# First query block built in halves, silu moved to GpSimd, and gate rows and second modulation columns back on TensorE, in a transformer block on one core

## The chip, the cores and the metric

The kernel runs on one core of a Trainium2 chip. The metric is the device time of one execution in microseconds; the median of several runs is compared.

## What is computed

```python
def _layernorm(x, axis=-1, eps=1e-05): ...           # (x - mean) / sqrt(var + eps)
x = A_x                                              # (1, 2048, 512) bf16
mod = (_silu(c) @ w_mod).reshape(c.shape[0], 6, 1, -1)   # c (1, 512), w_mod (512, 6*512)
sa, ca, ga, sb, cb, gb = ...                         # the six slices of mod
h = _layernorm(x) * (1 + ca) + sa
x = x + ga * attention(h)       # 32 query heads of 128, 8 kv heads, the last 512 cached keys, then wo
h = _layernorm(x) * (1 + cb) + sb
x = x + gb * (relu(h @ B_w1) @ B_w2)                 # 512 -> 1792 -> 512
```

The six slices of `mod` are needed in two shapes. `sa`, `ca`, `sb`, `cb` scale and shift the transposed activations, so they are wanted as columns (feature on the partition). `ga` and `gb` multiply rows of output, so they are wanted as one row repeated on all 128 partitions.

## The kernel before

The 2048 queries are handled in four blocks of 512 (`NB`), and each block has 32 heads. One pair (block, head) is a unit; there are 128 units and one step of the main loop for each. In step s the program issues, in this order: the tasks due at s (`run_tasks`), the scores of unit s for the first two key chunks (`s_mms(s, 0)`), the query projection of unit s + 2 (`q_mms`), the scores for the other two chunks, the product of probabilities and values of unit s - 1 (`pv_mms`), and up to four entries of a background queue (`pop_bg(4)` on `bgq`). An entry marked by `evac` ends a pop: it copies the finished bank `psW` (`WBK`) out on VectorE. The background queue holds the products with `wo`, which enter it for the first time at step 9, after eight heads. The MLP follows the last unit.

Every engine works through its own stream in program order. `KB.op` records an instruction with the semaphores it must wait for; `mm` and `tpose` (lines 1367 and 1370 of the profile) issue TensorE's matmuls and transposes. All loads are issued by SyncE (SP), apart from three early ones on ScalarE's queue. `load_wm01` brings the first two slices of `w_mod` as two halves of the contraction: chunks 0 and 1 on SP, chunks 2 and 3 on ScalarE's queue. `load_wm` brings slices 2 to 5, as tasks of steps 0 to 3.

The start of the program builds the first block. `silu_exp` transposes `c` on TensorE and takes exp(-c) on ScalarE. `ln_stat` takes mean and variance of tiles 0 to 2 on VectorE (tile 3 goes through ScalarE). `rstd_pow` takes the power -0.5 on GpSimd (POOL) for tiles 0 and 1, then for 2 and 3. `silu_mul` finishes silu on VectorE with three small instructions, and its result `sc_bf` feeds 32 matmuls of one column each (`mod_cols_mm(0)`), which give the first shift and scale columns `modc`. `ln_norm` normalizes tiles 0 to 2 on VectorE; tile 3 is normalized on ScalarE. Transposes (`ln_tposes`) bring all four tiles into banks 0 and 2, with 1, 2 and 3 filler matmuls (`warm`) between the tiles. `ln_mod_ps` then scales and shifts 512 queries at a time, two feature chunks on VectorE and two on ScalarE, into `hT[0]`, and `q_mms(0)`, `q_mms(1)` project them. `q_mms` ends with a copy of the bank to `qT` on ScalarE, for which the scores wait.

The gate rows (slices 2 and 5) and the second columns (slices 3 and 4) are made without TensorE: `mod_part` multiplies and adds the four chunks of a slice on VectorE (16 instructions, steps 5 to 33), `mod_sum` adds over the partitions on GpSimd (`partition_all_reduce`, four of them), and `mod_col` takes columns from the rows of slices 3 and 4 at step 48.

Of the kernel before, what the change touches and what calls it, by code (L numbers as in the profile page):

```python
# [8 lines left out]
ACTF = mybir.ActivationFunctionType  # L9
ALU = mybir.AluOpType  # L10
# [1188 lines left out]
def build_fast(nc, es, top, A_x, A_k_cache, A_v_cache, A_wq, A_wo, B_x, B_w1, B_w2, c, w_mod, out, flag):  # L1199
# [28 lines left out]
    def T(name, shape, dt=BF):  # L1228
        return es.enter_context(nc.sbuf_tensor(name, shape, dt))
# [26 lines left out]
    ones = T("ones", [P, P])  # L1256
    c_row = T("c_row", [DC, P])
    s3 = T("s3", [P, 4], F32)
    sc_bf = T("sc_bf", [P, DC])
    sc_f = T("sc_f", [P, DC], F32)  # L1260
    tmp = T("tmp", [P, DC], F32)
    modc = T("modc", [P, 4 * DC], F32)
    gaf = T("gaf", [P, D], F32)
    gbf = T("gbf", [P, D], F32)
    prv = h2T[1][:, :, :].rearrange("p c q -> p (c q)").bitcast(F32)
    pr = [gaf[:, :], prv[:, 0:D], prv[:, D:2 * D], gbf[:, :]]
    st = T("st", [P, NT, 6], F32)
    mv = T("mv", [P, NT, 2], F32)
    rstd = T("rstd", [P, NT], F32)
# [39 lines left out]
    R_xn, R_xnT = RL("xn", TPB), Res("xnT")  # L1309
    R_yt, R_yo = RL("yt", NY), RL("yo", NY)  # L1310
    R_b = RL("bank", 8)
    R_ident, R_ones, R_c, R_sc, R_scf, R_tmp, R_cst = (Res(n) for n in ("ident", "ones", "c", "sc", "scf", "tmp", "cst"))
    R_moda, R_modb, R_ga, R_gb = Res("moda"), Res("modb"), Res("ga"), Res("gb")
    R_pr = [R_ga] + RL("pr", 2) + [R_gb]
    R_st, R_mv, R_rstd = RL("st", NT), RL("mv", NT), RL("rstd", NT)
    R_s3, R_eps = Res("s3"), Res("eps")
    R_rinv, R_vmax, R_chk, R_good, R_flag = Res("rinv"), Res("vmax"), Res("chk"), Res("good"), Res("flag")
    R_h1 = [RL(f"h1_{i}_", FC) for i in range(2)]
# [53 lines left out]
    def warm(n):  # L1372
        for i in range(n):
            mm(bank[WBK], ones[:, :], ones[:, 0:1].to_broadcast([P, QB]), True, True, [R_ones], [WBK], i == n - 1)

    def ln_stat(t):
        kb.op(DVE, lambda e: e.bn_stats(st[:, t, :], x_sb[:, t, :]), reads=[R_x[t]], writes=[R_st[t]])  # L1377
        kb.op(DVE, lambda e: e.bn_aggr(mv[:, t, :], st[:, t, :]), reads=[R_st[t]], writes=[R_mv[t]])  # L1378
# [20 lines left out]

    def ln_tposes(tl, bks):  # L1400
        for cc in range(DC):
            bk = bks[cc // 2]
            o = (cc % 2) * 512 + tl * P
            tpose(bank[bk].bitcast(BF)[:, o:o + P], xn[:, tl, cc * P:(cc + 1) * P], [R_xn[tl]], [bk], cc == DC - 1)

    def ln_mod_ps(bks, dst, R_dst, which):
        o, r = (0, R_moda) if which == 1 else (2 * DC, R_modb)
        for k in range(2):
            for half, eng in ((0, DVE), (1, ACT)):
                cc = half * 2 + k  # L1410
                src = bank[bks[half]].bitcast(BF)[:, k * 512:(k + 1) * 512]
                sc, sh = modc[:, o + DC + cc:o + DC + cc + 1], modc[:, o + cc:o + cc + 1]
                if eng is DVE:
                    kb.op(DVE, lambda e, src=src, sc=sc, sh=sh, cc=cc: e.tensor_scalar(dst[:, cc, :], src, sc, sh, op0=ALU.mult, op1=ALU.add),
                          reads=[R_b[bks[half]], r], writes=[R_dst[cc]])
                else:
                    kb.op(ACT, lambda e, src=src, sc=sc, sh=sh, cc=cc: e.activation(dst[:, cc, :], src, ACTF.Identity, bias=sh, scale=sc),
                          reads=[R_b[bks[half]], r], writes=[R_dst[cc]])

    CC_ORDER = (0, 2, 1, 3)  # L1420
    QA = 2
# [1 line left out]
    def silu_exp(bk):  # L1423
        cT = bank[bk].bitcast(BF)[:, 0:DC]
        kb.op(PE, lambda e: e.transpose(cT, c_row[:, :], ident[0:DC, 0:DC]), reads=[R_c, R_ident], group_writes=[R_b[bk]])
        kb.op(ACT, lambda e: e.activation(tmp[:, :], cT, ACTF.Exp, scale=-1.0), reads=[R_b[bk]], writes=[R_tmp])

    def silu_mul(bk):
        cT = bank[bk].bitcast(BF)[:, 0:DC]
        kb.op(DVE, lambda e: e.tensor_scalar(tmp[:, :], tmp[:, :], 1.0, None, op0=ALU.add), reads=[R_tmp], writes=[R_tmp])  # L1430
        kb.op(DVE, lambda e: e.reciprocal(tmp[:, :], tmp[:, :]), reads=[R_tmp], writes=[R_tmp])
        kb.op(DVE, lambda e: e.tensor_tensor(sc_bf[:, :], cT, tmp[:, :], op=ALU.mult), reads=[R_tmp, R_b[bk]], writes=[R_sc])

    def mod_cols_mm(which, bk):
        fs = []
# [11 lines left out]
        kb.op(DVE, lambda e: e.tensor_copy(modc[:, mo:mo + DC], bank[bk][:, :DC]), reads=[R_b[bk]], writes=[r])  # L1447
        kb.op(DVE, lambda e: e.tensor_scalar(modc[:, mo + DC:mo + 2 * DC], bank[bk][:, DC:2 * DC], 1.0, None, op0=ALU.add), reads=[R_b[bk]], writes=[r])

    def mod_part(sl, cc):  # L1450
        dst, r = pr[sl - 2], R_pr[sl - 2]
        if cc == 0:
            kb.op(DVE, lambda e: e.tensor_scalar(dst, wm[sl][:, 0, :], sc_f[:, 0:1], None, op0=ALU.mult), reads=[R_wm[sl], R_scf], writes=[r])
        else:
            kb.op(DVE, lambda e: e.scalar_tensor_tensor(dst, wm[sl][:, cc, :], sc_f[:, cc:cc + 1], dst, op0=ALU.mult, op1=ALU.add),
                  reads=[R_wm[sl], R_scf, r], writes=[r])

    def mod_sum(sl):
        src, rs = pr[sl - 2], R_pr[sl - 2]
        kb.op(POOL, lambda e: e.partition_all_reduce(src, src, P, bass_isa.ReduceOp.add), reads=[rs], writes=[rs])  # L1460

    def mod_col(sl):
        src, rs = pr[sl - 2], R_pr[sl - 2]
        o = 2 * DC + (sl - 3) * DC
        v = src.rearrange("p (c j) -> p c j", c=DC)
        kb.op(DVE, lambda e: e.tensor_tensor(v, v, ident[:, :].unsqueeze(1).to_broadcast([P, DC, P]), op=ALU.mult), reads=[rs, R_ident], writes=[rs])
        kb.op(DVE, lambda e: e.tensor_reduce(modc[:, o:o + DC], v, axis=AX.X, op=ALU.add), reads=[rs], writes=[R_modb])
        if sl == 4:
            kb.op(DVE, lambda e: e.tensor_scalar(modc[:, o:o + DC], modc[:, o:o + DC], 1.0, None, op0=ALU.add), reads=[R_modb], writes=[R_modb])

    bgq = deque()

# [13 lines left out]

    def q_mms(u, bk=QBK):
        b, h = units[u]
        order = CC_ORDER if u < QA else range(DC)
        for i, cc in enumerate(order):  # L1490
            mm(bank[bk], wq_sb[:, cc, h * Dh:(h + 1) * Dh], hT[b % 2][:, cc, :], i == 0, i == DC - 1,
               [R_wq[h], R_hT[b % 2][cc]], [bk], i == DC - 1)
        kb.op(ACT, lambda e: e.activation(qT[u % NQT][:, :], bank[bk], ACTF.Copy), reads=[R_b[bk]], writes=[R_qT[u % NQT]])  # L1493

    def s_mms(u, pr):
# [50 lines left out]
    def add(step, fn):  # L1546
        tasks.append((step, len(tasks), fn))
        tasks.sort(key=lambda x: x[:2])
# [18 lines left out]
    for i in range(2):  # L1567
# [10 lines left out]
    kb.op(POOL, lambda e: e.affine_select(ident[:, :], ones[:, :], pattern=[[1, P]], compare_op=ALU.is_equal, fill=0.0,  # L1578
                                          base=0, channel_multiplier=-1), reads=[R_ones], writes=[R_ident])
    kb.op(POOL, lambda e: e.memset(cst[:, 1:2], eps), writes=[R_eps])  # L1580
    kb.op(POOL, lambda e: e.memset(v_sb[:, :, :, P:VW], 1.0), writes=[R_v1])
    kb.op(ACT, lambda e: e.activation(cst[:, 2:3], cst[:, 0:1], ACTF.Exp), reads=[R_cst], writes=[Res("dummy")])
    warm(7)
    silu_exp(5)
    warm(9)
    t3 = TPB - 1
    kb.op(ACT, lambda e: e.activation(xn[:, t3, :], x_sb[:, t3, :], ACTF.Copy, accum_out=s3[:, 0:1]), reads=[R_x[t3]], writes=[R_xn[t3], R_s3])
    kb.op(ACT, lambda e: e.activation(s3[:, 1:2], s3[:, 0:1], ACTF.Copy, scale=-1.0 / D), reads=[R_s3], writes=[R_s3])
# [6 lines left out]
    def rstd_pow(lo, hi):  # L1595
        kb.op(POOL, lambda e: e.tensor_tensor(rstd[:, lo:hi], rstd[:, lo:hi], cst[:, 0:1].to_broadcast([P, hi - lo]), op=ALU.pow),
              reads=R_rstd[lo:hi] + [R_cst], writes=R_rstd[lo:hi])

    ln_stat(0)
    ln_stat(1)  # L1600
    rstd_add(0, 2)
# [1 line left out]
    ln_stat(2)  # L1603
    rstd_add(2, 3)
    rstd_pow(2, 4)
    silu_mul(5)
    for tl in range(3):
        ln_norm(tl)
    kb.op(ACT, lambda e: e.activation(s3[:, 3:4], s3[:, 1:2], ACTF.Copy, scale=rstd[:, t3:t3 + 1]), reads=[R_s3, R_rstd[t3]], writes=[R_s3])
    kb.op(ACT, lambda e: e.activation(xn[:, t3, :], x_sb[:, t3, :], ACTF.Identity, scale=rstd[:, t3:t3 + 1], bias=s3[:, 3:4]),  # L1610
          reads=[R_x[t3], R_rstd[t3], R_s3], writes=[R_xn[t3]])
    fs = mod_cols_mm(0, QBK)
    for f in fs[:len(fs) // 2]:
        f()
    ln_tposes(0, [0, 2])
    for f in fs[len(fs) // 2:]:
        f()
    mod_cols_evac(0, QBK)
    for tl in range(1, TPB):
        ln_tposes(tl, [0, 2])  # L1620
        warm(tl)
    ln_mod_ps([0, 2], hT[0], R_hT[0], 1)
    load_wq(R, R)
    load_k(1)
    load_v(1)
    q_mms(0)
    q_mms(1, 5)
    kb.op(DVE, lambda e: e.tensor_copy(sc_f[:, :], sc_bf[:, :]), reads=[R_sc], writes=[R_scf])


    for g in range(2, G):
# [14 lines left out]
    for i, s in enumerate([s for s in range(57, NU) if s % HQ in (1, 2, 3, 4)][:FC]):  # L1646
        add(s, lambda i=i: load_mlp(i))

    for sl, steps in ((2, (5, 6, 7, 9)), (3, (10, 11, 13, 14)), (4, (15, 25, 26, 27)), (5, (29, 30, 31, 33))):
        for cc, s in enumerate(steps):  # L1650
            add(s, lambda sl=sl, cc=cc: mod_part(sl, cc))
    for sl, s in ((2, 10), (3, 27), (4, 38), (5, 105)):
        add(s, lambda sl=sl: mod_sum(sl))
    for sl in (3, 4):
        add(48, lambda sl=sl: mod_col(sl))

    for s in range(NU):
        run_tasks(s, 100)
        if wo_ready and wo_ready[0][0] <= s:
            _, b_, j_ = wo_ready.popleft()  # L1660
            enqueue_wo(b_, j_)
        s_mms(s, 0)
        if s + QA < NU:
            q_mms(s + QA)
        s_mms(s, 1)
        if s >= 1:
            pv_mms(s - 1)
        pop_bg(4)
# [192 lines left out]
```

## Time and profile before

| | |
|---|---|
| median of 5 runs | 563.67 us (562.63 to 564.29) |
| the profiled execution | 563.22 us, of which its span 561.5 us |
| TensorE busy (matmuls, modelled ends) | 554.8 us, 99% of the span |
| ScalarE, VectorE, GpSimd busy | 350.3, 252.4 and 51.8 us |
| DMA, mean over the span | 76 GB/s; 256 GB/s in the first fortieth |
| granted TensorE clock | 1.0 |

Busy time is the sum over an engine's instructions in one profiled execution. A matmul row's duration includes its way through the array, and consecutive matmuls overlap, so their pace is read from the distance of their starts. In a wait's row, the name after the arrow is what the waiting instruction was released by.

### The profile page before, as it was taken

How to read it: one execution, taken by the hardware profiler on the slowest of the kernel's cores; microseconds unless marked ns; L12 is line 12 of the kernel's file. 1: busy time of each engine (PE TensorE's matmuls, PEld its weight loads, DVE VectorE, ACT ScalarE, POOL GpSimd, SP SyncE). 2: the span in 40 equal slices, each digit the busy share in tenths (PEclk: the TensorE clock that was granted, in tenths of full speed). 3: DMA queues.
4: the chain of work that ended last, by engine and by line, in shares of the span. 5: the costliest groups of instructions: out<-in, count | busy, mean ns of one | idle time of the engine just before them, and what ended most of it. 6: DMA issues, size and time to landing. Idle time of an engine off the chain costs nothing.

```text
span 561.5 us, 9730 instructions
## 1 busy us (share of the span) xinstructions
PE 554.8 (99%) x4132; PEld 314.7 (56%) x4132; DVE 252.4 (45%) x550; ACT 350.3 (62%) x453; POOL 51.8 (9%) x46
## 2 busy tenths in 40 slices
PE   7999999999999999999999999999999999999998
PEld 3565555555555555555555555555555654444444
DVE  3455556543336745333347453333354448321134
ACT  4986666666666666666666666666666644432500
POOL 1020002003230000033000000332000000000000
DMA  9899666512232156243532531121214210210001
GB/s 256 209 187 193 146 163 95 113 39 38 39 76 39 39 88 137 55 98 57 132 57 57 85 63 39 39 38 39 39 39 72 44 28 1 42 35 23 21 29 47
DMA packets 113308, 42.66 MB, mean 76 GB/s; under 512 B 93928, under 2 KB 112104, under 8 KB 113256
## 3 DMA queue, kind: packets, MB, share of 16 engines
q1 hardware_dynamic: 112024, 40.82, 36.2%
q10 hardware_dynamic: 1232, 1.15, 0.6%
q8 instruction: 33, 0.54, 0.4%
q14 instruction: 19, 0.16, 0.1%
HBM read 18.35 MB, written 2.10 MB: 36 GB/s over the span
## 4 chain that ended last, share of the span: by engine, by line
PE 95%; DMA 3%; DVE 1%; issue 0%; DVEq 0%
PE psS L1367 28%; PE psO L1367 26%; PE psQ L1367 22%; PE psW L1367 19%; DMA xnT<-xn 2%; DMA x<-in_A_x_dram 1%; DVE st L1377 0%; DVE o L1512 0%; DVE xn L1388 0%; PE psS L1370 0%; DVE mv L1378 0%; DVE rstd L1593 0%; DVE PT L1691 0%; DVE PT L1693 0%; DVE rinv L1511 0%
## 5 line engine op out<-in xcount | busy, mean ns | idle before, releaser
L1501 ACT ACTIVATE PT<-psS 128x1024 bf16<-128x1024 f32 x256 | 262.6, 1028 | 128.2 <-PE psS L1367 128.2
L1367 PE MATMUL psS<-qT,kT 128*128 128x512 bf16 x512 | 151.8, 379 | 0.0
L1367 PEld LDWEIGHTS psO<-v,PT 128*128 128x128 bf16 x2048 | 126.3, 98 | 31.8 <-DVE o L1512 2.5
L1367 PE MATMUL psO<-v,PT 128*128 128x129 bf16 x2048 | 137.0, 220 | 0.6 <-DVE o L1512 0.5
L1367 PE MATMUL psQ<-hT,wq 128*128 128x512 bf16 x508 | 130.5, 379 | 0.1
L1367 PE MATMUL psW<-wo,oT 128*128 128x512 bf16 x512 | 130.6, 379 | 0.0
L1511 DVE RECIPROCAL rinv<-psO 128x4 f32<-128x4 f32 x128 | 23.3, 182 | 216.0 <-PE psO L1367 216.0
L1512 DVE TENSOR_TENSOR o<-psO,rinv 128x512 bf16<-128x512 f32 x128 | 88.5, 691 | 4.7 <-DVE rinv L1511 0.3
L1367 PEld LDWEIGHTS psQ<-hT,wq 128*128 128x128 bf16 x508 | 49.6, 98 | 60.7 <-issue 0.5
L1367 PEld LDWEIGHTS psS<-qT,kT 128*128 128x128 bf16 x512 | 49.5, 98 | 58.9 <-ACT PT L1501 0.7
L1493 ACT ACTIVATE qT<-psQ 128x512 bf16<-128x512 f32 x127 | 75.2, 592 | 0.5 <-PE psQ L1367 0.5
L1680 ACT ACTIVATE wq<-psS 128x512 bf16<-128x512 f32 x56 | 33.4, 597 | 49.5 <-PE psS L1367 49.5
L1367 PEld LDWEIGHTS psW<-wo,oT 128*128 128x128 bf16 x512 | 44.9, 98 | 32.9 <-DVE acc L1534 1.2
L1534 DVE TENSOR_TENSOR acc<-psW,acc 128x512 f32<-128x512 f32 x48 | 33.1, 691 | 6.7 <-PE psW L1367 6.7
L1367 PE MATMUL psO<-wmw,wq 128*128 128x512 bf16 (+1 forms) x168 | 32.9, 352 | 0.0
L1537 POOL TENSOR_TENSOR acc<-acc,gaf 128x512 f32<-128x512 f32 x12 | 15.2, 1268 | 158.0 <-DVE acc L1534 150.7
L1383 POOL TENSOR_TENSOR rstd<-rstd,cst 128x4 f32<-128x4 f32 x7 | 7.2, 1035 | 213.1 <-DVE rstd L1382 213.1
L1691 DVE TENSOR_TENSOR PT<-psO,gbf 128x512 f32<-128x512 f32 (+1 forms) x12 | 7.5, 624 | 40.4 <-PE psO L1367 40.4
L1367 PE MATMUL psS<-h2T,wmw 128*128 128x512 bf16 x112 | 25.3, 379 | 0.0
L1367 PEld LDWEIGHTS psO<-wmw,wq 128*128 128x128 bf16 x168 | 15.3, 98 | 16.5
L1367 PE MATMUL psS<-hT,wmw 128*128 128x512 bf16 x112 | 24.5, 379 | 0.0
L1377 DVE BATCH_NORM_STATS2 st<-x 128x6 f32<-128x512 bf16 x31 | 21.0, 678 | 5.1 <-DMA x<-in_A_x_dram 5.1
(77 smaller groups left out, 190.1 us busy)
## 6 DMA issues: line engine op xcount, KB each, us to landing
wo<-in_A_wo_dram SPq DMA_DIRECT2D x4, 1024.0 KB, 6.8
wq<-in_A_wq_dram SPq DMA_DIRECT2D x7, 512.0 KB, 5.7
wmw<-in_B_w_dram SPq DMA_DIRECT2D x14, 256.0 KB, 3.0
wmw<-in_w_mod_dram SPq DMA_DIRECT2D x5, 512.0 KB, 4.7
oT<-o SPq DMA_TRANSPOSE x128, 2.4
out_dram<-PT SPq DMA_DIRECT2D x15, 128.0 KB, 1.7
x<-in_A_x_dram SPq DMA_DIRECT2D x3, 512.0 KB, 4.1
v<-in_A_v_cache_dram SPq DMA_DIRECT2D x8, 128.0 KB, 4.8
```

The lines of the kernel that those rows point to most:

```text
L1367: kb.op(PE, lambda e: e.matmul(out_ap, lhsT, rhs, start=start, stop=stop), reads=reads, group_writes=[R_b[k] for k in bk], signal=signal)
L1377: kb.op(DVE, lambda e: e.bn_stats(st[:, t, :], x_sb[:, t, :]), reads=[R_x[t]], writes=[R_st[t]])
L1383: kb.op(POOL, lambda e: e.tensor_tensor(rstd[:, sl], rstd[:, sl], cst[:, 0:1].to_broadcast([P, hi - lo]), op=ALU.pow), reads=R_rstd[sl] + ...
L1493: kb.op(ACT, lambda e: e.activation(qT[u % NQT][:, :], bank[bk], ACTF.Copy), reads=[R_b[bk]], writes=[R_qT[u % NQT]])
L1501: kb.op(ACT, lambda e: e.activation(PT[u % NPT][:, pr * 2:pr * 2 + 2, :], s_ps[pr][:, :, :], ACTF.Exp, scale=scale), reads=[R_b[pr * 2], R ...
L1511: kb.op(DVE, lambda e: e.reciprocal(rinv[:, u, :], o_ps[:, :, P]), reads=[R_b[5], R_b[6]], writes=[R_rinv])
L1512: kb.op(DVE, lambda e: e.tensor_tensor(o_sb[u % NOS][:, :, :], o_ps[:, :, 0:P], rinv[:, u, :].unsqueeze(2).to_broadcast([P, TPB, P]), op=A ...
L1534: kb.op(DVE, lambda e: e.tensor_tensor(acc[:, tl, :], bank[WBK], acc[:, tl, :], op=ALU.add), reads=[R_b[WBK], R_acc[tl]], writes=[R_acc[tl]])
L1537: kb.op(eng, lambda e: e.tensor_tensor(acc[:, tl, :], acc[:, tl, :], gaf[:, :], op=ALU.mult), reads=[R_acc[tl], R_ga], writes=[R_acc[tl]])
L1680: kb.op(ACT, lambda e: e.activation(h1T[b % 2][:, fc, :], bank[bk], ACTF.Relu), reads=[R_b[bk]], writes=[R_h1[b % 2][fc]], pre=all_events( ...
L1691: kb.op(DVE, lambda e: e.tensor_tensor(yt[i][:, c0:c1], bank[bk][:, c0:c1], gbf[:, c0:c1], op=ALU.mult), reads=[R_b[bk], R_gb], writes=[R_ ...
```

## The change

The silu: exp(-c) stays on ScalarE, which also copies the transposed `c` to `c_f`. GpSimd then takes min and add, the power -1, and the product with `c_f`, and these three stand ahead of `rstd_pow` on its stream.

The first block: tile 3 is normalized on GpSimd by one `tensor_scalar`. The 32 column matmuls are issued ahead of all transposes. Tiles 0 and 1 (half 0) are transposed, then scaled and shifted in pieces of 256 queries, and the first three chunks of unit 0's projection of that half follow. Tile 2 is normalized on VectorE after the two pieces of half 0 there. Tiles 3 and 2 (half 1) are transposed into other banks, scaled and shifted (three pieces on VectorE, one on ScalarE), and the projections of units 0 and 1 are completed. One filler matmul stands after the transposes of half 0, and eight instead of nine after `silu_exp`.

The second modulation columns and the gate rows: the GpSimd sums and VectorE parts are gone. In step 4, `mods2` puts 8 matmuls of 512 columns (stationary `sc_rep`, silu of `c` repeated over 128 columns), 32 matmuls of one column, and their three copies by VectorE into the background queue.

```diff
-    sc_f = T("sc_f", [P, DC], F32)
+    c_f = T("c_f", [P, DC], F32)
+    sc_rep = T("sc_rep", [P, DC, P])
...
-    def silu_mul(bk):
-        cT = bank[bk].bitcast(BF)[:, 0:DC]
-        kb.op(DVE, ... tensor_scalar(tmp, tmp, 1.0, None, op0=ALU.add))
-        kb.op(DVE, ... reciprocal(tmp, tmp))
-        kb.op(DVE, ... tensor_tensor(sc_bf, cT, tmp, op=ALU.mult))
+        kb.op(ACT, ... activation(c_f, cT, ACTF.Copy))            # last line of silu_exp
+    def silu_mul():
+        kb.op(POOL, ... tensor_scalar(tmp, tmp, 1e38, 1.0, op0=ALU.min, op1=ALU.add))
+        kb.op(POOL, ... tensor_tensor(tmp, tmp, cst[:, 3:4] ..., op=ALU.pow))   # cst[:, 3] = -1.0
+        kb.op(POOL, ... tensor_tensor(sc_bf, c_f, tmp, op=ALU.mult))
...
-    def mod_part(sl, cc): ...
-    def mod_sum(sl): ...
-    def mod_col(sl): ...
+    def mod_row(j):
+        sl, dst, r = (2, gaf, R_ga) if j == 0 else (5, gbf, R_gb)
+        for cc in range(DC):
+            bgq.append(lambda cc=cc: mm(bank[WBK], sc_rep[:, cc, :], wm[sl][:, cc, :], cc == 0, cc == DC - 1, [R_screp, R_wm[sl]], [WBK], cc == DC - 1))
+        evac(lambda: kb.op(DVE, lambda e: e.tensor_copy(dst[:, :], bank[WBK]), reads=[R_b[WBK]], writes=[r]))
...
-    warm(9)
+    warm(8)
...
+    silu_mul()
     ln_stat(0)
     ln_stat(1)
     rstd_add(0, 2)
...
     rstd_pow(2, 4)
-    silu_mul(5)
-    for tl in range(3):
-        ln_norm(tl)
-    kb.op(ACT, ... activation(s3[:, 3:4], s3[:, 1:2], ACTF.Copy, scale=rstd[:, t3:t3 + 1]))
-    kb.op(ACT, ... activation(xn[:, t3, :], x_sb[:, t3, :], ACTF.Identity, scale=rstd[:, t3:t3 + 1], bias=s3[:, 3:4]))
+    ln_norm(0)
+    ln_norm(1)
+    kb.op(POOL, ... tensor_scalar(xn[:, t3, :], x_sb[:, t3, :], s3[:, 1:2], rstd[:, t3:t3 + 1], op0=ALU.add, op1=ALU.mult))
-    fs = mod_cols_mm(0, QBK)
-    for f in fs[:len(fs) // 2]:
-        f()
-    ln_tposes(0, [0, 2])
-    for f in fs[len(fs) // 2:]:
+    for f in mod_cols_mm(0, QBK):
         f()
     mod_cols_evac(0, QBK)
-    for tl in range(1, TPB):
-        ln_tposes(tl, [0, 2])
-        warm(tl)
-    ln_mod_ps([0, 2], hT[0], R_hT[0], 1)
+    ln_tposes(0, TB[0])
+    ln_tposes(1, TB[0])
+    warm(1)
+    mod_half(0, 0, DVE)
+    mod_half(0, 2, ACT)
+    mod_half(0, 1, DVE)
+    mod_half(0, 3, ACT)
+    ln_norm(2)
+    q_half(0, 0, CC_ORDER[:3], QBK)
+    ln_tposes(3, TB[1])
+    ln_tposes(2, TB[1])
+    q_half(0, 0, CC_ORDER[3:], QBK)
+    mod_half(1, 0, DVE)
+    mod_half(1, 2, ACT)
+    mod_half(1, 1, DVE)
+    mod_half(1, 3, DVE)
+    q_half(1, 0, CC_ORDER, 5)
+    for u, bk in ((0, QBK), (1, 5)):
+        q_half(u, 1, CC_ORDER, bk)
+        q_evac(u, bk)
...
-    q_mms(0)
-    q_mms(1, 5)
-    kb.op(DVE, ... tensor_copy(sc_f, sc_bf))
+    kb.op(DVE, ... tensor_copy(sc_rep, sc_bf[:, :].unsqueeze(2).to_broadcast([P, DC, P])))
...
+    def mods2():
+        mod_row(0)
+        fs = mod_cols_mm(1, WBK)
+        bgq.append(lambda: [f() for f in fs] and None)
+        evac(lambda: mod_cols_evac(1, WBK))
+        mod_row(1)
...
+        if s == 4:
+            mods2()
```

`mod_half` is one scale-and-shift of 128 features by 256 queries from a bank to `hT[0]`; `q_half` is `q_mms` for 256 queries without its copy, and `q_evac` is that copy. `CC_ORDER` is (0, 2, 1, 3).

More of the change, by code (lines that the diff above doesn't have):

```diff
@@ L1264, in build_fast @@
     gbf = T("gbf", [P, D], F32)
-    prv = h2T[1][:, :, :].rearrange("p c q -> p (c q)").bitcast(F32)
-    pr = [gaf[:, :], prv[:, 0:D], prv[:, D:2 * D], gbf[:, :]]
     st = T("st", [P, NT, 6], F32)
@@ L1311, in build_fast @@
     R_b = RL("bank", 8)
-    R_ident, R_ones, R_c, R_sc, R_scf, R_tmp, R_cst = (Res(n) for n in ("ident", "ones", "c", "sc", "scf", "tmp", "cst"))
+    R_ident, R_ones, R_c, R_sc, R_screp, R_tmp, R_cst = (Res(n) for n in ("ident", "ones", "c", "sc", "screp", "tmp", "cst"))
     R_moda, R_modb, R_ga, R_gb = Res("moda"), Res("modb"), Res("ga"), Res("gb")
-    R_pr = [R_ga] + RL("pr", 2) + [R_gb]
     R_st, R_mv, R_rstd = RL("st", NT), RL("mv", NT), RL("rstd", NT)
+    R_h0 = RL("h0", DC)
+    R_cf = Res("cf")
     R_s3, R_eps = Res("s3"), Res("eps")
@@ L1401, in ln_tposes @@
         for cc in range(DC):
-            bk = bks[cc // 2]
+            bk = bks[cc]
             o = (cc % 2) * 512 + tl * P
             tpose(bank[bk].bitcast(BF)[:, o:o + P], xn[:, tl, cc * P:(cc + 1) * P], [R_xn[tl]], [bk], cc == DC - 1)
[L1406 to L1418, printed above, removed]
     CC_ORDER = (0, 2, 1, 3)
@@ L1426, in silu_exp @@
         kb.op(ACT, lambda e: e.activation(tmp[:, :], cT, ACTF.Exp, scale=-1.0), reads=[R_b[bk]], writes=[R_tmp])
-    def silu_mul(bk):
-        cT = bank[bk].bitcast(BF)[:, 0:DC]
-        kb.op(DVE, lambda e: e.tensor_scalar(tmp[:, :], tmp[:, :], 1.0, None, op0=ALU.add), reads=[R_tmp], writes=[R_tmp])
-        kb.op(DVE, lambda e: e.reciprocal(tmp[:, :], tmp[:, :]), reads=[R_tmp], writes=[R_tmp])
-        kb.op(DVE, lambda e: e.tensor_tensor(sc_bf[:, :], cT, tmp[:, :], op=ALU.mult), reads=[R_tmp, R_b[bk]], writes=[R_sc])
+        kb.op(ACT, lambda e: e.activation(c_f[:, :], cT, ACTF.Copy), reads=[R_b[bk]], writes=[R_cf])
+    def silu_mul():
+        kb.op(POOL, lambda e: e.tensor_scalar(tmp[:, :], tmp[:, :], 1e38, 1.0, op0=ALU.min, op1=ALU.add), reads=[R_tmp], writes=[R_tmp])
+        kb.op(POOL, lambda e: e.tensor_tensor(tmp[:, :], tmp[:, :], cst[:, 3:4].to_broadcast([P, DC]), op=ALU.pow), reads=[R_tmp, R_eps], writes=[R_tmp])
+        kb.op(POOL, lambda e: e.tensor_tensor(sc_bf[:, :], c_f[:, :], tmp[:, :], op=ALU.mult), reads=[R_tmp, R_cf], writes=[R_sc])
     def mod_cols_mm(which, bk):
@@ L1448, in mod_cols_evac @@
         kb.op(DVE, lambda e: e.tensor_scalar(modc[:, mo + DC:mo + 2 * DC], bank[bk][:, DC:2 * DC], 1.0, None, op0=ALU.add), reads=[R_b[bk]], writes=[r])
[L1450 to L1469, printed above, removed]
+    def mod_row(j):
[3 more added lines that the diff above has]
+        evac(lambda: kb.op(DVE, lambda e: e.tensor_copy(dst[:, :], bank[WBK]), reads=[R_b[WBK]], writes=[r]))
     bgq = deque()
@@ L1488, in q_mms, with q_evac @@
         b, h = units[u]
-        order = CC_ORDER if u < QA else range(DC)
-        for i, cc in enumerate(order):
+        for i, cc in enumerate(range(DC)):
             mm(bank[bk], wq_sb[:, cc, h * Dh:(h + 1) * Dh], hT[b % 2][:, cc, :], i == 0, i == DC - 1,
-               [R_wq[h], R_hT[b % 2][cc]], [bk], i == DC - 1)
+               [R_wq[h], R_hT[b % 2][cc]] + ([R_h0[cc]] if b == 0 else []), [bk], i == DC - 1)
+        q_evac(u, bk)
+    def q_evac(u, bk=QBK):
         kb.op(ACT, lambda e: e.activation(qT[u % NQT][:, :], bank[bk], ACTF.Copy), reads=[R_b[bk]], writes=[R_qT[u % NQT]])
@@ L1580, in build_fast @@
     kb.op(POOL, lambda e: e.memset(cst[:, 1:2], eps), writes=[R_eps])
+    kb.op(POOL, lambda e: e.memset(cst[:, 3:4], -1.0), writes=[R_eps])
     kb.op(POOL, lambda e: e.memset(v_sb[:, :, :, P:VW], 1.0), writes=[R_v1])
@@ L1605, in build_fast @@
     rstd_pow(2, 4)
-    silu_mul(5)
-    for tl in range(3):
-        ln_norm(tl)
-    kb.op(ACT, lambda e: e.activation(s3[:, 3:4], s3[:, 1:2], ACTF.Copy, scale=rstd[:, t3:t3 + 1]), reads=[R_s3, R_rstd[t3]], writes=[R_s3])
-    kb.op(ACT, lambda e: e.activation(xn[:, t3, :], x_sb[:, t3, :], ACTF.Identity, scale=rstd[:, t3:t3 + 1], bias=s3[:, 3:4]),
-          reads=[R_x[t3], R_rstd[t3], R_s3], writes=[R_xn[t3]])
-    fs = mod_cols_mm(0, QBK)
-    for f in fs[:len(fs) // 2]:
-        f()
-    ln_tposes(0, [0, 2])
@@ L1616, in build_fast @@
-    for f in fs[len(fs) // 2:]:
+    ln_norm(0)
+    ln_norm(1)
+    kb.op(POOL, lambda e: e.tensor_scalar(xn[:, t3, :], x_sb[:, t3, :], s3[:, 1:2], rstd[:, t3:t3 + 1], op0=ALU.add, op1=ALU.mult),
+          reads=[R_x[t3], R_rstd[t3], R_s3], writes=[R_xn[t3]])
+    for f in mod_cols_mm(0, QBK):
         f()
     mod_cols_evac(0, QBK)
-    for tl in range(1, TPB):
-        ln_tposes(tl, [0, 2])
-        warm(tl)
-    ln_mod_ps([0, 2], hT[0], R_hT[0], 1)
+    HB = QB // 2
+    R_half = [R_h0, R_hT[0]]
@@ new lines, in build_fast, with mod_half @@
+    TB = [[0, 0, 2, 2], [1, 1, 3, 6]]
+    def mod_half(hf, cc, eng):
+        bk = TB[hf][cc]
+        o = (cc % 2) * 512 + hf * HB
+        src, dst = bank[bk].bitcast(BF)[:, o:o + HB], hT[0][:, cc, hf * HB:(hf + 1) * HB]
+        sc, sh = modc[:, DC + cc:DC + cc + 1], modc[:, cc:cc + 1]
+        if eng is DVE:
+            kb.op(DVE, lambda e: e.tensor_scalar(dst, src, sc, sh, op0=ALU.mult, op1=ALU.add), reads=[R_b[bk], R_moda], writes=[R_half[hf][cc]])
+        else:
+            kb.op(ACT, lambda e: e.activation(dst, src, ACTF.Identity, bias=sh, scale=sc), reads=[R_b[bk], R_moda], writes=[R_half[hf][cc]])
@@ new lines, in q_half @@
+    def q_half(u, hf, order, bk):
+        for cc in order:
+            mm(bank[bk][:, hf * HB:(hf + 1) * HB], wq_sb[:, cc, u * Dh:(u + 1) * Dh], hT[0][:, cc, hf * HB:(hf + 1) * HB], cc == CC_ORDER[0], cc == CC_ORDER[-1],
+               [R_wq[u], R_half[hf][cc]], [bk], cc == CC_ORDER[-1])
+    ln_tposes(0, TB[0])
[7 more added lines that the diff above has]
+    q_half(0, 0, CC_ORDER[:3], QBK)
@@ L1623, in build_fast @@
+    ln_tposes(3, TB[1])
[8 more added lines that the diff above has]
+        q_half(u, 1, CC_ORDER, bk)
+        q_evac(u, bk)
     load_wq(R, R)
@@ L1625, in build_fast @@
     load_v(1)
-    q_mms(0)
-    q_mms(1, 5)
-    kb.op(DVE, lambda e: e.tensor_copy(sc_f[:, :], sc_bf[:, :]), reads=[R_sc], writes=[R_scf])
+    kb.op(DVE, lambda e: e.tensor_copy(sc_rep[:, :, :], sc_bf[:, :].unsqueeze(2).to_broadcast([P, DC, P])), reads=[R_sc], writes=[R_screp])
     for g in range(2, G):
@@ L1647, in build_fast @@
         add(s, lambda i=i: load_mlp(i))
[L1649 to L1655, printed above, removed]
+    def mods2():
[4 more added lines that the diff above has]
+        mod_row(1)
     for s in range(NU):
         run_tasks(s, 100)
+        if s == 4:
+            mods2()
         if wo_ready and wo_ready[0][0] <= s:
```

## The prediction

> **What bounds the kernel now.** I read the page's engine shares and chain first, then a table by stretches, then TensorE's waits, then the first 14 us in order of time, and last the landing times of the first loads.
>
> ```profile
> span 561.5 us, 9730 instructions
> PE 554.8 (99%) x4132; PEld 314.7 (56%) x4132; DVE 252.4 (45%) x550; ACT 350.3 (62%) x453; POOL 51.8 (9%) x46
> PE 95%; DMA 3%; DVE 1%; issue 0%; DVEq 0%
> ```
>
> TensorE carries 95% of the chain that ended last. A busy share alone could hide gaps, so I look at the steps in which the changed work lies (24 to 34 us holds steps 4 to 7):
>
> ```profile
> 24.00:34.00 10.00, 10.00 (x95) 6.46 (x94) 6.20 (x12) 9.27 (x12) 0.00 (x0) 1.00 1.19 206
> 34.00:60.00 26.00, 26.00 (x216) 15.61 (x214) 15.20 (x29) 19.18 (x25) 3.25 (x1) 1.00 1.03 200
> ```
>
> The columns after the stretch are its length and the busy time of PE, PEld, DVE, ACT and POOL, then the clock. TensorE has no hole here: the chain in order of time steps from matmul to matmul without a gap from 23.64 to beyond 39 us, 2.63 us a step. The waits of TensorE over the whole span:
>
> ```profile
> PE psQ L1367 <- DVE sc_bf L1432: 1.3, 1, 1.3
> PE psW L1367 <- POOL cst L1577: 1.0, 1, 1.0
> PE psO L1425 <- DMA c_row<-in_c_dram: 0.8, 1, 0.8
> PE psO L1367 <- DVE o L1512: 0.5, 2, 0.3
> ```
>
> Three of the four lie before 9 us; the fourth (2 times, 0.5 us in all) is after 200 us, and the DVE and POOL work that this change removes ends at 176 us, apart from one GpSimd sum at 383 us. So only two things can move the end: when the scores of unit 0 begin (13.75 us), and how much TensorE does after that. The start in order of time, TensorE's rows first, then VectorE's, then ScalarE's:
>
> ```profile
> 8.53 0.55 PE L1367 MATMUL psQ<-sc_bf,wmw 128*128 128x1 bf16 x16 [1.32 <-DVE sc_bf L1432]
> 8.94 0.38 PE L1370 MATMUL psS<-ident,xn 128*128 128x128 bf16 x4
> 9.16 0.54 PE L1367 MATMUL psQ<-sc_bf,wmw 128*128 128x1 bf16 x16
> 9.56 0.38 PE L1370 MATMUL psS<-ident,xn 128*128 128x128 bf16 x4
> ...
> 10.66 0.38 PE L1370 MATMUL psS<-ident,xn 128*128 128x128 bf16 x4
> ...
> 13.75 0.59 PE L1367 MATMUL psS<-qT,kT 128*128 128x512 bf16 x2
> ```
>
> ```profile
> 8.38 1.05 DVE L1388 TENSOR_SCALAR xn<-x,mv,rstd 128x512 bf16<-128x512 bf16 x3
> 9.74 0.16 DVE L1447 COPY modc<-psQ 128x4 f32<-128x4 f32 x1 [0.31 <-PE psQ L1367]
> ...
> 11.08 0.99 DVE L1414 TENSOR_SCALAR hT<-psS,modc 128x512 bf16<-128x512 bf16 x2 [0.99 <-PE psS L1370]
> ```
>
> ```profile
> 11.08 1.45 ACT L1417 ACTIVATE hT<-psS,modc 128x512 bf16<-128x512 bf16 x2 [1.08 <-PE psS L1370]
> 13.01 0.60 ACT L1493 ACTIVATE qT<-psQ 128x512 bf16<-128x512 f32 x1 [0.48 <-PE psQ L1367]
> ```
>
> The reader is to see the relay: columns from 8.53, last transposes at 10.66, scale and shift 0.42 us later at 11.08, the copy of unit 0's queries at 13.01, scores 0.74 us after that. The page puts the first wait down to `sc_bf`. Another releaser stands right behind it, the first half of `w_mod` on SP's queue, issued at 1.65 us:
>
> ```profile
> L1301 SPq DMA_DIRECT2D wmw<-in_w_mod_dram x1: 413/413/413, 1.7 to 1.7; - x1
> DMA to landing us min/median/max: 6.6/6.6/6.6
> ```
>
> It lands at 1.65 + 6.6 = 8.25 us, and the first column matmul reads chunk 0 out of it.
>
> **Matmuls added to the steps.** Gate rows: 8 matmuls of 512 columns. The chain in order of time shows eight such `psW` matmuls in 1.73 us. Second columns: 32 matmuls of one column; starts at 8.53 and 8.94, and at 9.16 and 9.56, give 0.41 and 0.40 us for 16, so 0.81 us (bounds 0.76 by the chain's 0.38 for 16, 1.10 by the 0.55 of a row with its tail). Sum 2.54 us, all on the path, because steps 4, 5 and 6 have no hole. Their background slots hold nothing else (the first `wo` matmul is at 39.45). Would they wait, too? They need slice 2 at the end of step 4 (26.3 us in the old clock), slices 3 and 4 at 28.9, slice 5 at 31.6. Landings: 10.2 + 4.7 = 14.9, 13.5 + 6.9 = 20.4, 20.6 + 4.2 = 24.8, 23.2 + 4.7 = 27.9 us. Nothing waits; were one late, TensorE's whole stream would stand behind it. `sc_rep` is one VectorE copy of 128x512, at most the 0.69 us of the `acc` copy, at about 12 us with VectorE's next work near 18 us: nothing. The bank's copies to `gaf` and `gbf` (0.69 us each) and `modc` (2 of 0.16) have until the next step's background slot, 1.7 us away.
>
> **Work removed.** VectorE loses 16 parts (12 of 0.74, 3 of 0.48, one of 0.77 us) and about 2.9 us of `mod_col`, GpSimd four sums of 3.25 us. TensorE waited for neither between 24 and 200 us: gain 0. Bounds: at most the 0.5 us of waits on `o` after 200 us, at least 0.
>
> **The start, piece by piece.** Silu: exp ends at 5.35. GpSimd's power of 128x2 took 0.72 to 0.76 and of 128x4 1.02 us. The min-and-add and the product have no row; bounds 0.10 (a memset of one column) and 1.02 (the power), I take 0.3, near the 0.29 of the `ident` select. So `sc_bf` is ready at 5.43 + 0.3 + 1.02 + 0.3 + gaps of 0.1 = 7.15 us, 1.3 earlier than now. But the weights land at 8.25: the columns begin at 8.30, 0.23 earlier, and the other 1.1 us is lost to the load. GpSimd's queue behind silu: the first `rstd_pow` moves from 7.07 to 7.2, done 7.94; tiles 0 and 1 are normalized 8.0 to 8.72 (starts 0.32 apart as now), before TensorE wants them at 9.1. The second power ends at 8.75 and tile 3 follows. Its price has no row: below, the `ident` select's 0.29 us for 128 elements grown to 512 is 1.2; the two-input product of 128x512 f32 is 1.27; a one-input bf16 operation may be less, 0.5. With any of these it is done by 10.1; it is wanted at 10.6. ScalarE gains one 0.17 us copy and loses 0.29 + 0.81; neither is on the path.
>
> [...]
>
> Now TensorE: 32 columns from 8.30 take 0.81, so transposes of tile 0 at 9.11 and tile 1 at 9.33; the last column's result is evacuated from about 9.30 and `modc` stands at 9.66. Half 0 can be scaled from 9.33 + 0.42 = 9.75. A half piece has no row. VectorE: 128x4 takes 0.16 and 128x512 from the bank 0.54, so 256 elements 0.35, starts 0.25 apart. ScalarE: 0.29 for one element with column operands, 0.78 for 512, so 0.53, starts 0.43 apart. VectorE's pieces end at 10.10 and 10.35, tile 2 at 10.65; ScalarE's at 10.28 and 10.71. Projection of three chunks (0.11 us each) waits for them until 10.57; transposes of tile 3 follow, those of tile 2 start at 10.79; half 1 is scaled from 10.79 + 0.42 = 11.21. VectorE has three pieces there, ending 11.56, 11.81, 12.06; ScalarE's ends 11.74. Unit 0's last matmul starts at 12.13, is out after 0.27 (the 128x256 row of the last MLP tile) and the copy starts at 12.43. Scores follow 0.74 later, at 13.17 against 13.75: gain 0.58. Bounds: pieces at exactly half the whole ones' time give 0.8; pieces that cost as much as whole ones put the copy at about 13.4, a loss of 0.4. I keep 0.55, since the fixed share is seen in the 128x4 rows.
>
> **Sum.** 2.54 - 0.55 = 2.0 us, with own ends 1.7 and 2.9. The profiled execution took 563.22 us (span 561.5 and 1.7 around it) and would take 565.2. It lies 0.45 below the median of 563.67; on the median the forecast is 565.7, 0.35% slower, against the 0.2% (1.1 us) that a measurement of this kernel can tell.
>
> **Rivals.**
> - *No measurable difference: the start gains over 1.4 us.* Place: the column matmuls. If the first weights land by 7.2 us, the columns run at once, and the copies of `modc` wait only for tile 1 (8.72): the half is scaled 0.6 earlier, and with the cheapest pieces the gain is 0.8 + 0.6 = 1.4. Price: +1.1 or a little less, 564.7. It decides from the point where the first scores start at 12.35 or before. Against it: the landing at 8.25 and the fixed share of small pieces. Chance 0.13.
> - *GpSimd is late.* If the two small operations cost 1.02 each, `sc_bf` comes at 8.6, tile 1 at 10.1, and `modc` 0.8 us later than above: +2.8, 566.5. Chance 0.06.
> - *The clock drops.* The seven fillers at the start took 3.17 us, later ones 0.22 each: the array starts at half pace. Six fillers between 9.7 and 11.7 us become one. TensorE's waits now reach 1.3 us without a drop; the new ones are estimated at 1.3 and below 0.5. A drop as long as those 3.2 us at half pace would add 1.6: +3.6, 567.3. Chance 0.04. [...]
> - *The removed work was a brake that the waits don't show,* on memory or on queues: over 3.1 us would have to come back for a faster kernel. Against it: matmuls of 379 ns everywhere, beside GpSimd's sums too. 562.5 us; chance 0.06.
>
> **How the numbers follow.** The forecast has 0.71. Slower: 0.71 + 0.06 + 0.04 = 0.81; same 0.13; faster 0.06. The range goes from 564.4 (the first rival, less 0.3 for the spread of the runs) to 566.9 (own end +2.9, plus 0.3), and leaves out the clock, the hidden brake and a part of the rest.
>
> **What would show it.** In the changed profile: the first column matmul near 8.3 us with the load of `w_mod` as its releaser, not `sc_bf`; tile 3 on GpSimd done before its transposes; first scores near 13.2; steps 4 to 6 longer by 0.86, 0.81 and 0.86 us, all others as now. It is wrong if the scores start before 12.4 or after 13.8, if those steps grow by less than 2.3 us together, or if waits on `o` disappear elsewhere.

## The result and the profile after

The changed kernel takes 564.09 us (median of 25 runs, 563.48 to 565.18) against 563.25 us for the kernel before (45 runs): 1.0015 times as long, 95% interval 1.0009 to 1.0020. That is 0.84 us slower, where the forecast added 2.0 us. Slower was right; the size was wrong, and the time lies below the range of 564.4 to 566.9. The forecast's 565.7 also stood on the median of five runs of the kernel before (563.67); over 45 runs this median is 563.25, so 0.4 us of the miss of 1.6 is the base.

The page of the changed kernel, to set beside that of before:

```profile
span 562.4 us, 9784 instructions
PE 555.7 (99%) x4174; PEld 316.9 (56%) x4174; DVE 242.5 (43%) x533; ACT 349.4 (62%) x453; POOL 41.1 (7%) x47
PE 98%; DMA 1%; issue 0%; DVE 0%; SPq 0%; ACT 0%
```

TensorE has 42 matmuls more, VectorE and GpSimd are some 10 us less busy, and the share of DMA in the chain fell from 3% to 1%. That last line is the one to remember. TensorE's waits over the whole span:

```profile
PE psQ L1367 <- DMA wmw<-in_w_mod_dram: 1.2, 1, 1.2
...
PE psO L1411 <- DMA c_row<-in_c_dram: 0.6, 1, 0.6
...
PE psS L1367 <- ACT qT L1466: 0.3, 1, 0.3
```

The start, TensorE first, then GpSimd, then VectorE:

```profile
8.02 0.94 PE L1367 MATMUL psQ<-sc_bf,wmw 128*128 128x1 bf16 x32 [1.21 <-DMA wmw<-in_w_mod_dram]
8.82 0.61 PE L1370 MATMUL psS<-ident,xn 128*128 128x128 bf16 x8
...
13.19 0.59 PE L1367 MATMUL psS<-qT,kT 128*128 128x512 bf16 x2 [0.34 <-ACT qT L1466]
```

```profile
5.27 0.23 POOL L1416 TENSOR_SCALAR tmp<-tmp 128x4 f32<-128x4 f32 x1 [3.46 <-ACT c_f L1413]
5.59 1.04 POOL L1417 TENSOR_TENSOR tmp<-tmp,cst 128x4 f32<-128x4 f32 x1
6.71 0.20 POOL L1418 TENSOR_TENSOR sc_bf<-c_f,tmp 128x4 bf16<-128x4 f32 x1
...
8.67 0.77 POOL L1583 TENSOR_SCALAR xn<-x,s,rstd 128x512 bf16<-128x512 bf16 x1
```

```profile
9.47 0.73 DVE L1598 TENSOR_SCALAR hT<-psS,modc 128x256 bf16<-128x256 bf16 x2
...
11.03 0.73 DVE L1598 TENSOR_SCALAR hT<-psS,modc 128x256 bf16<-128x256 bf16 x2 [0.51 <-PE psO L1370]
11.67 0.40 DVE L1598 TENSOR_SCALAR hT<-psO,modc 128x256 bf16<-128x256 bf16 x1
```

The wait for the weights, GpSimd's prices and the first scores (13.19) come out close to what was worked out (the scores by luck, see below). So do the steps with the new matmuls, in the chain in order of time:

```profile
25.72 0.86 PE psW L1367 x4
...
29.21 0.78 PE psW L1367 x32
...
32.65 0.86 PE psW L1367 x4
```

0.86 + 0.78 + 0.86 = 2.50 us. I compared the start of each unit's reciprocal (line 1511 before, 1484 after) in the two traces. The changed kernel is 0.56 us ahead at unit 0, 1.96 behind from unit 6 on, as forecast; then 1.30 behind after unit 58 and 0.69 behind after unit 90. So 1.27 us is given back between 205 and 330 us, where the change has no line. (The spans differ by 0.9 us; the other 0.2 us arises after the last unit, where the twelve profiles scatter by as much.) There VectorE's timeline has, before and then after:

```profile
205.05 0.73 DVE L1388 TENSOR_SCALAR xn<-x,mv,rstd 128x512 bf16<-128x512 bf16 x2 [3.81 <-DMA xnT<-xn]
205.70 0.17 DVE L1511 RECIPROCAL rinv<-psO 128x4 f32<-128x4 f32 x1
205.91 0.69 DVE L1512 TENSOR_TENSOR o<-psO,rinv 128x512 bf16<-128x512 f32 x1
```

```profile
205.44 0.74 DVE L1388 TENSOR_SCALAR xn<-x,mv,rstd 128x512 bf16<-128x512 bf16 x2 [2.24 <-DMA xnT<-xn]
```

VectorE stands at a normalization that may not overwrite `xn` before the transpose DMA `xnT` has read it. The division of a unit's output (`rinv`, `o`) is queued behind, and TensorE waits for its bank. With the wait of 2.24 us TensorE does not wait; with 3.81 it does, as the chain before shows:

```profile
199.06 5.90 DMA xnT<-xn
...
205.91 0.70 DVE o L1512
206.62 0.05 issue
206.66 1.08 PE psO L1367 x16
```

The issue of that DMA and its landing, before and then after:

```profile
L1300 SPq DMA_TRANSPOSE xnT<-xn x1: 1927/1927/1927, 199.1 to 199.1; - x1
...
DMA to landing us min/median/max: 5.9/5.9/5.9
```

```profile
L1299 SPq DMA_TRANSPOSE xnT<-xn x1: 1941/1941/1941, 201.0 to 201.0; - x1
...
DMA to landing us min/median/max: 4.3/4.3/4.3
```

The waits from 30 to 450 us, before and after:

```profile
DVE xn L1388 <- DMA xnT<-xn: 7.6, 2, 3.8
DVE hT L1396 <- DMA xnT<-xn: 7.1, 2, 3.6
PEld psO L1367 <- DVE o L1512: 2.5, 4, 0.8
PE psO L1367 <- DVE o L1512: 0.5, 2, 0.3
```

```profile
DVE hT L1396 <- DMA xnT<-xn: 4.9, 2, 2.5
DVE xn L1388 <- DMA xnT<-xn: 4.5, 2, 2.3
```

Why did the same transfer take 5.9 us in one kernel and 4.3 in the other? The page has a DMA queue of kind "instruction", q8: 33 packets, 0.54 MB. The packet records of the trace show packets of 16384 bytes on it. In the main loop of the kernel before there is about one in 16 us; in the 25 stretches between the packets at 43.88 and 444.22 us TensorE starts 217 to 299 instructions (mostly 244 to 270, 256 on average), weight loads counted. In the kernel before, one such packet starts at 203.07 (0.88 us long) and one at 315.48 (0.96), inside the transfers of 199.06 to 204.96 and 311.62 to 317.46; 4-byte packets of the transpose that started beside the first took 632 ns on average instead of some 8. In the changed kernel they start at 199.3 and 311.2, before the transfers. (The transfer issued at 87.16 us is hit in the kernel before, too, and lands in 6.2 us; TensorE has no wait there.)

**Theory A**: as there is one packet to some 256 TensorE instructions, their place against the steps is set by how many of these instructions lie ahead. The 84 more of the change moved them out of the transfers, and this gave back 1.27 us. **Theory B**: the removed VectorE and GpSimd work was a brake. **Theory C**: long landings are scatter of single executions.

### The profile page after: what moved, and what is told of

It reads as the page before. It is cut to its first block, busy times and chain, and to the rows that moved or that the text cites. A ratio compares the mean times of both kernels' runs of the same rounds, so it can differ in the third digit from the quotient of the medians.

```text
span 562.4 us, 9784 instructions
## 1 busy us (share of the span) xinstructions
PE 555.7 (99%) x4174; PEld 316.9 (56%) x4174; DVE 242.5 (43%) x533; ACT 349.4 (62%) x453; POOL 41.1 (7%) x47
## 4 chain that ended last, share of the span: by engine, by line
PE 98%; DMA 1%; issue 0%; DVE 0%; SPq 0%; ACT 0%
PE psS L1367 28%; PE psO L1367 26%; PE psQ L1367 23%; PE psW L1367 20%; DMA wmw<-in_w_mod_dram 1%; PE psS L1370 0%; SPq L1300 0%; ACT qT L1466 0%; DVE hT L1598 0%; DVE PT L1694 0%; DVE PT L1696 0%; PE psO L1370 0%
## 5 line engine op out<-in xcount | busy, mean ns | idle before, releaser
L1367 PE MATMUL psQ<-hT,wq 128*128 128x512 bf16 (+1 forms) x512 | 131.0, 377 | 0.4 <-DVE hT L1598 0.4
```

Of the source, the lines that this page charges most:

```text
L1367: kb.op(PE, lambda e: e.matmul(out_ap, lhsT, rhs, start=start, stop=stop), reads=reads, group_writes=[R_b[k] for k in bk], signal=signal)
```

## Experiments

**Move the packets in the kernel before.** Nothing but the fillers ahead of the loop is changed:

```diff
-    warm(9)
+    thin(51, 90)      # 51 fillers of 90 columns
```

> The kernel before with one edit: the nine filler matmuls of 512 columns after the transpose of c become 51 of 90 columns, so TensorE's stream has 42 matmuls (84 instructions with their weight loads) more ahead of the main loop, as in the changed kernel, at nearly the same time (51 x 0.040 = 2.04 us against 1.94) and ahead of a wait of 1.3 us. Theory A (the 16384-byte packets of DMA queue 8, one per about 256 TensorE instructions, hit the transposes xnT at 203 and 315 us in the kernel before and miss them in the changed one): the packets move by about 5 us against the steps, xnT lands in 4.3 us instead of 5.9, the waits of TensorE on o vanish, time 563.25 - 1.27 = 562.0. Theory B (the removed VectorE and GpSimd work was the brake): nothing moves, 563.2. Theory C (the long landings are scatter of single executions): 563.2 and long landings in some profiles of either kernel.

Measured: 561.88 us, 0.9977 of the kernel before (0.9968 to 0.9986), that is -1.3 us. Its packet starts at 197.6, ahead of the transfer, every `xnT` lands in 4.3 or 4.4 us, and the waits of TensorE on `o` are gone. From 30 to 450 us:

```profile
DVE hT L1400 <- DMA xnT<-xn: 5.0, 2, 2.5
DVE xn L1392 <- DMA xnT<-xn: 4.6, 2, 2.3
```

**Move them back in the changed kernel.**

```diff
-    warm(8)
+    thin(94, 44)
```

> The changed kernel with one edit: the eight filler matmuls of 512 columns become 94 of 44 columns, 86 matmuls or 172 instructions more, which with the 84 of the change make 256, one whole period of the packets of queue 8. They fill 94 x 0.03 = 2.8 us at most and end before the first weights land near 7.9 us. Theory A: the packets stand to the steps as in the kernel before, xnT lands in 5.9 us at some of its issues, the waits on o come back, time 564.09 + 1.27 = 565.4. Theories B and C: 564.1.

Measured: 565.22 us, 1.0039 (1.0025 to 1.0053) of the kernel before; 1.1 us more than the changed kernel. The packets start at 205.54 and 318.13, inside the transfers, which land in 6.0 us; the waits are back:

```profile
DVE xn L1392 <- DMA xnT<-xn: 7.8, 2, 3.9
...
PEld psO L1367 <- DVE o L1489: 2.8, 4, 0.9
```

565.22 is 0.39% above before; the prediction, which left the packets out, had 0.35% for the change.

In both kernels the thin fillers were slower in the profile than expected: 90 columns took 0.07 us, not 0.040, and the 51 of them held TensorE to 8.75 us, past the landing of the weights at 7.95; the 94 held it to 8.35 (weights at 7.92). So both times may contain a later start; the comparison unit by unit at the end of this section does not.

**Take GpSimd's sums out of the kernel before.**

```diff
-    for sl, s in ((2, 10), (3, 27), (4, 38), (5, 105)):
-        add(s, lambda sl=sl: mod_sum(sl))
```

> The kernel before without its four GpSimd sums over partitions (the gate rows and second columns are then one partition's share only); TensorE's stream is the same. Theory A: 563.25, the packets and the long landings stay. Theory B, if the sums were the brake: 562.0 to 562.6. Theory C: 563.25.

Measured: 563.29 us, 1.0005 (0.9996 to 1.0014): no change, and landings of 5.9 us at the same two places. Theory B falls for the sums, and by the two runs above it falls altogether: the loss goes while all that work is still there, and it comes back in the kernel that has none of it. That A's three numbers came within 0.2 us (with starts later than assumed in two of the three, so in part by luck) and that the landings follow the packets in every profile leaves nothing for C.

**The rows alone.** The kernel before with `mod_part`, `mod_sum` and `mod_col` replaced by `mod_row` and `mods2`.

> The kernel before, in which only the gate rows and the second modulation columns go back to TensorE (the start is that of before). 40 matmuls more, 80 instructions. Theory A: +2.5 for the matmuls in steps 4 to 6, -1.27 for the packets that now miss: 564.5. Theory B: the same 564.5, since the VectorE and GpSimd work is gone here too. Neither holds, and the start alone saves more than its 0.56: 565.8.

Measured: 564.07 us, 1.0019 (1.0010 to 1.0028), +1.0 us, with the expected +1.2 inside the interval. Landings of 4.3 to 4.4 us, no wait on `o`. It also costs what the whole change costs, which points to a new start that is worth little.

**Half the shift.**

```diff
-    warm(9)
+    thin(30, 152)
```

> The kernel before with 30 fillers of 152 columns in place of nine of 512: 21 matmuls or 42 instructions more, half the shift of e1_before_shifted. The packets move by about 2.6 us against the steps, to about 200.5 and 312.9, early in the time in which xnT is under way. Theory A as far as known: any hit inside the transfer holds it up, long landings stay, 563.1. If only a hit near its end matters: 562.0.

Measured: 562.00 us, 0.9985 (0.9976 to 0.9994). The expectation was half right. The packets start at 200.5 and 311.8, early in the transfers, and landings are 5.4 and 5.2 us:

```profile
L1300 SPq DMA_TRANSPOSE xnT<-xn x1: 3342/3342/3342, 198.7 to 198.7; - x1
...
  DVE xn L1392: 3.3, 1
...
DMA to landing us min/median/max: 5.4/5.4/5.4
```

So a hit early in the transfer delayed its landing by 1 us and a late one by 1.6. But most of the loss is gone already: VectorE's wait falls from 3.8 to 3.3 us, TensorE's weight loads wait 1.1 us instead of 2.5. This fits a division with some slack, of which only the excess reaches TensorE.

**The start alone.** The changed start with rows and columns made as before.

> The changed kernel's start, with the gate rows and second columns made by VectorE and GpSimd as before. TensorE's stream has 2 matmuls more than the kernel before, so the packets of queue 8 stay where they are. Theory A: 0.55 less than before by the earlier scores, xnT lands in 5.9 us twice, 562.5. If the start were worth more than its scores' time shows: 562.0 or less.

Measured: 562.97 against 562.94, 1.0004 (0.9995 to 1.0013). The forecast -0.55 lies outside the interval; the landings are long at the same places (5.9 and 5.8 us). **With the packets out of the way:**

> As e3_start_alone, with 40 matmuls more ahead of the loop (the eight fillers of 512 columns become 48 of 85), so that the packets of queue 8 miss the transposes. Theory A: both gains, 563.1 - 0.55 - 1.27 = 561.3, faster than the kernel before and the changed one. If the two gains are the same one: 561.9.

Measured: 561.22 us, 0.9971 (0.9960 to 0.9982), the fastest version: 1.7 us faster than the kernel before, 2.9 than the changed one. To separate its two gains, the pair was run side by side:

> The same kernel as e1_before_shifted (start of before, packets out of the way), beside e10 in one call, to measure the start alone where no packet disturbs. By the starts of the scores so far (13.2 to 14.0 us with the start of before, 13.1 to 13.6 with the changed start) the start is worth 0.2 us, not the 0.55 of the prediction: 561.7 here and 561.5 for e10. By the prediction: 561.7 and 561.15.

> The same kernel as e6_start_and_shift (changed start, rows as before, packets out of the way). With a start worth 0.2 us: 0.2 less than e9. With the prediction's 0.55: 0.55 less than e9.

Measured: 561.60 (0.9974, 0.9964 to 0.9985) and 561.21 us (0.9969, 0.9959 to 0.9980). The difference of 0.4 lies between the two expectations and well inside the intervals. All four pairs (rows alone against the whole change, start alone against before, and the shifted kernels twice) put the start between a loss of 0.2 and a gain of 0.4 us; closer it could not be settled. In the last pair's profiles the thin fillers held the columns to 8.82 and 8.36 us, past the weights at 7.96 and 7.87, so it does not measure the start undisturbed either.

**Silu back on VectorE in the changed kernel.**

```diff
-    kb.op(POOL, ... tensor_scalar / pow / tensor_tensor)       # silu_mul()
+    kb.op(DVE, ... tensor_scalar / reciprocal / tensor_tensor) # silu_mul(5), after rstd_pow(2, 4)
```

> The changed kernel with silu's last three instructions on VectorE as before. The step of the prediction: moving silu to GpSimd gains only what is left until the first weights land. sc_bf then comes at about 8.4, the columns start 0.4 us later than in the changed kernel, scores too: 564.1 + 0.4 = 564.5. If the move were worth its whole 1.1 us: 565.2. If it is covered altogether: 564.1.

Measured: 564.17 us, 1.0017 (1.0008 to 1.0026), not told apart from the changed kernel's 1.0015. In its profile `sc_bf` stands 0.2 us after the first weights landed (7.92 and 7.71; 0.15 to 0.29 us in the six profiles with the start of before), and the columns waited for the fillers until 8.30 anyway. So the load covers all of the move but 0.2 to 0.3 us; the expected 0.4 took the load's scatter for a gain.

**All profiles, unit by unit.** As above for the changed kernel, each trace can be set against that of the kernel before by the starts of the reciprocals, here from unit 8 to unit 91, which leaves out the start and the added matmuls. The seven profiles whose two `xnT` (near 200 and 312 us) land in 4.3 or 4.4 us (the changed kernel, the kernel before with moved packets twice, rows alone, the new start with moved packets twice, and silu on VectorE) gain 1.28 us each. Half the shift gains 1.06. The three others in which both land in 5.8 to 6.0 us lie between a gain of 0.04 and a loss of 0.22.

## Why the prediction was right and wrong

- **Matmuls added**: forecast 2.54, measured 2.50 in the chain. Right, and nothing waited for slices or `sc_rep`.
- **GpSimd**: small operations 0.23 and 0.20 (taken 0.3), tile 3 in 0.77 us (0.5 to 1.27). The page names the load as the releaser, as forecast, and tile 3 is done at 9.44, before its transposes at 10.38.
- **The start**: the scores at 13.19 met the forecast 13.17 by luck, by two errors that cancel. The weights landed at 7.89, not 8.23, since the profiled execution of before had a late first load: its `x` landed at 5.05 us, in the other eleven profiles at 4.51 to 4.82. And a half piece costs VectorE 0.40 to 0.41 us, 0.32 apart (taken 0.35 and 0.25), ScalarE 0.55 to 0.56 (0.53). Counted from the landing of `x`, the scores start 8.70 us later in each of the four profiles with before's start and fillers at full pace when the weights came, 8.50 and 8.45 with the new start: the term is 0.2 to 0.25, not 0.55. Where the fillers were still at half pace when the weights came, both starts were later (9.21 and 9.40 with before's start, 8.83 to 9.47 with the new one), so its size is open within the runs' -0.2 to 0.4. I measured a gain against one execution's clock time where only its distance from the load carries over.
- **Work removed, and "only two things can move the end"**: here the step failed. It put the gain between 24 and 200 us at 0 and after 200 us at 0.5 at most, and called all other steps unchanged. The runs show 1.27 us given back after 205 us, not by the removed work but by the place of the instruction packets against two transfers. The bound was TensorE's row alone; its matmul ends are modelled, and the weight loads' row of the same waits has 2.5 us. The view of the chain that I showed said DMA 3%, and the page's next line has `xnT` with 2%: a transfer stood in the chain, and I asked only whether the change touches the work that waits there. It touches TensorE's instruction count, which places the packets: with 84 instructions more ahead of the loop, the one at 203.07 us started at 197.6.
- **Rivals**: none named this. The hidden brake was nearest in its effect (waits on `o` go), but its cause, the removed work, was not it. The text's own test "if waits on `o` disappear elsewhere" is what happened.

With the measured terms: 2.50 - 0.2 - 1.27 = 1.0 us, inside the interval of 0.5 to 1.1.

What the packets cost lay in their place. In the changed kernel, with 35 of them over the span against 33, the view shows no wait of TensorE from 30 to 450 us; in the kernel before two of them delay transfers on whose readers TensorE then waits, which costs 1.3 us. That their place follows TensorE's instruction count is shown by the shifted kernels (197.6 us with 84 instructions more, 200.5 with 42); what they carry is not shown.

## What to carry to other kernels

When a bound kernel moves by less than the work added to it, align the two traces unit by unit: the place where the distance changes leads to the cause, even where the diff has no line. Read a stall from the weight loads' waits as well as the matmuls', and look at each DMA in the chain for slack, since a delay there is hidden only as far as its readers have slack: here a landing 1.6 us late cost 0.6 to 0.7 us each time. Compare a change of a few tenths per cent also against a version with the same count of instructions per engine (fillers in an idle place, which must end before the wait there does), or what is measured may be where the instruction packets fall.

## What was not expected of the hardware

- A 16384-byte instruction packet inside a transpose DMA of 4.3 us delayed its landing by 0.9 to 1.1 us when it started 1.0 to 1.8 us after the issue, and by 1.5 to 1.8 us when it started 3.9 to 4.3 us after it. In twelve profiles it is the only difference found between short and long landings in the main loop.
- The array reached full pace at different moments in different executions. Fillers of 512 columns start 0.22 us apart from 5 us on in some profiles, but 0.43 apart until 6.8 us in the two profiles with rows alone and without the sums, and until 7.9 in the one of the start alone. In the profile with silu on VectorE the eight transposes are still at half pace, 0.107 us apart instead of 0.055:

```profile
9.20 1.01 PE L1370 MATMUL psS<-ident,xn 128*128 128x128 bf16 x8
```

  Scores then start at 13.97 us instead of 13.2 (14.00 in the second profile of start and shift, which has the same pace there). The granted clock reads 1.0 in these stretches as in the fast ones, so the profile does not show the clock as the cause. What sets the moment is not shown; in the twelve profiles it lies anywhere from 5 us to after 9.9 us. This makes the start, and a gain of 0.2 us in it, hard to measure.
